# Two bursts of attention matmuls for each unit, and TensorE in the order in which the program is written

## The chip, the cores and the metric

The kernel runs on one core of a Trainium2 chip. The metric is device time in microseconds (us) of one execution: 988.76 us, the median of three runs (986.52 to 989.58). Five engines work side by side, each through its own queue in order: TensorE (PE in the profile, its weight loads PEld), VectorE (DVE), ScalarE (ACT), GpSimd (POOL) and SyncE (SP), which here issues the DMAs.

## The reference

Three stages follow each other on 3072 tokens (4 sequences of 768). Weights come as float64, everything else is float32.

```python
# attention: B, H, S, D = 4, 8, 768, 48; a state of 48x48 for each head, decayed channel by channel
for t in range(S):
    cur = einsum('bhd,bhe->bhde', u * k[t], v[t])
    y[t] = einsum('bhd,bhde->bhe', r[t], state + cur)
    state = w[t][..., None] * state + einsum('bhd,bhe->bhde', k[t], v[t])
x = y as [3072, 384]
x = ((x @ w1) * (x @ w2)) @ w3 @ w_out          # layer one: 384 -> 1024 -> 384
h = x @ w_in                                     # layer two: 384 -> 2048 -> 384
out = (h * clip(h + 3, 0, 6) / 6) @ w_out2
```

## The kernel before, in words

**Products.** A product of full precision is split into three matmuls of fp32r: high by high, high by low, low by high (`mm3`, L118 to L121). So almost every matmul of the trace has one of the lines L119, L120 and L121; its moving side has 384 columns in layer one and 512 in layer two. "A product" below is nine such matmuls, three for each 128 rows of the contraction.

**Start (0 to 116.6 us).** w3 and w_out are multiplied into one matrix (w34, L375) while the float64 words of the weights are turned into float32 by integer arithmetic on DVE, ACT and POOL (`conv`, `split`). The first units of attention run beside that.

**Attention** is cut into 32 units: a pair of heads, half a sequence, three chunks of 128 tokens. Head 0 of a pair lies on partitions 0 to 47, head 1 on 64 to 111. For unit m:

- `load(m)`: two DMAs, `wkr` (decays, k, r by channel) and `rkv` (r, k, v by token), into three buffers each; the load of unit m+2 waits until unit m-1, which had the buffer, is done.
- `prep(m)`: DVE scans the products of decays forwards (`e`, L154) and backwards (`f`, L158) and multiplies r and k by them (L168, L165); POOL and DVE make the diagonal of the scores (`A`).
- `do_kn`: PE transposes k (L186, "T" below). `do_sc(m, j)`: the scores of head j, three matmuls of 48 rows (L195, "SC"), which DVE then copies under a mask into `A` (copy_predicated, L196).
- `do_kv`: the update of the state (L206, "KV"), 128 rows and 48 columns for each head and chunk; then a scan over the chunks on DVE (`s`, L213).
- `do_y(m-1)`, one unit late: for each chunk, the masked products v by A (L228, "YA", 128 rows, 48 columns) and then r by the state (L231, "YS", 48 rows, 48 columns) on top of them, in one bank. A unit of a sequence's first half has no state in its first chunk, so it has two chunks of YS; one of the second half has three. y goes to `xt` in two or three DMAs.

The PSUM banks `abank` (three) go round: T, SC of head 0, SC of head 1, YA and YS, KV. So KV takes the bank that head 0's scores leave when copy_predicated has read them.

**Layer one (116.6 to about 583 us)** goes through eight blocks of 384 tokens. For each of eight feature tiles f there are two products into banks 0 and 1 (`ab`, weights w12), an elementwise product (`a`, L474), its split into `gh` and `gl`, and then `out1` for the tile before: nine matmuls into banks 2 to 4. Between these products, steps of attention for the next block are pulled: after each product the quota grows by 0.3 (0.5 in block 6), and each full one emits a whole unit's step, until the next block's four units are done. After feature tile 3 of block 6 attention is over; its memory goes to the weights of layer two (`win_start`), which are converted until layer two begins.

**Layer two** goes through six blocks of 512 tokens and 16 feature tiles: one product into bank 0 or 1, Relu on ACT, a multiplication on DVE, the split, and `out2` for the tile before (L506).

**What sets the order.** The kernel is built with a scheduler that simulates the engines and puts each engine's instructions into the order in which they come free there. It moves matmuls past each other: attention's matmuls stand in pieces between the products.

The DMA queue has one order too: SP issues loads, writes of y to `xt` and the rest, and waits at its head.

Of the kernel before, what the change touches and what calls it, by code (L numbers as in the profile page):

```python
# [16 lines left out]
NP = H // 2            # head pairs  # L17
T1 = S // 2            # tokens of a block of the first layer: half a sequence
NM = B * 2 * NP        # units of attention: a head pair, half a sequence
C = 128                # chunk of the recurrence  # L20
NC = T1 // C           # chunks in a unit
ZC = C + 1
WZ = NC * ZC + 1       # decay columns, with a zero column around each chunk
PR = 112               # head 0 of a pair on partitions 0..47, head 1 on 64..111
NS = NC + 2            # columns of the state scan: reset, carried state, chunks
# [3 lines left out]
T2 = 512               # tokens of a block of the second layer  # L29
NB2 = B * S // T2  # L30
NT = B * S
# limits of float64's upper word read as float32, for the two ways of conversion
# [4 lines left out]
TINY = 1e-25           # least product of decays within a chunk; less is held there and told by its reciprocal  # L37
FAR = 1e13             # largest reciprocal of a chunk's product of decays
PACE, PACE6 = 0.3, 0.5  # steps of attention for each product of the first layer; in its block 6
FW = 3                 # feature tile of block 6 after which attention's memory goes to the second layer  # L40


def pool_split(bi, f):
    """Where Pool takes a product's low part from the vector engine, which converts weights then."""
    return bi in (0, 1, 7) and f % 2 and f < 7


def build(nc, tc, a):
# [23 lines left out]
    count = cst.tile([1, 1], I32, name="count")  # L72
    half = cst.tile([128, 1], F32, name="half")
# [16 lines left out]
    # ------------------------------------------------------------ weights  # L90
    def conv(f, raw, late, mixed):
        """float64 words to float32, cut to 24 bits, in two stages; exponents beyond float32's are limited."""
# [30 lines left out]
    # ------------------------------------------------------------ attention  # L123
# [66 lines left out]
    def do_sc(m, j):  # L190
        d = un[m]
        ps = psum_a()[:, :T1].rearrange("p (c t) -> p c t", t=C)
        for c in range(NC):
            t = slice(C * c, C * c + C)
            mm(ps[:, c], d["k"][rows[j], t], d["r"][rows[j], t], start=True, stop=True)  # L195
        V.copy_predicated(d["A"][:, j], mask.unsqueeze(1).to_broadcast([128, NC, C]), ps)  # L196
# [23 lines left out]
    def do_y(m):  # L220
# [3 lines left out]
        pc = c3(ps)  # L224
        for c in range(NC):
            st = h > 0 or c > 0
            for j in range(2):
                mm(pc[rows[j], c], d["v"][:, c, j], d["A"][:, j, c], start=True, stop=not st)  # L228
            if st:
                for j in range(2):  # L230
                    mm(pc[rows[j], c], d["s"][rows[j], :, c + 1], d["r"][rows[j], C * c:C * c + C], start=False,  # L231
                       stop=True)
# [11 lines left out]
    def attention():  # L244
        for m in range(NM + 1):
            nxt = prep(m + 1) if m + 1 < NM else iter(())
            if m < NM:
                do_kn(m)
                next(nxt, None)
                do_sc(m, 0)  # L250
                do_sc(m, 1)
                next(nxt, None)
            if m + 2 < NM:
                load(m + 2)
            next(nxt, None)
            if m > 0:
                do_y(m - 1)
            if m < NM:
                do_kv(m)
            next(nxt, None)  # L260
            yield 4 * m + 4
# [4 lines left out]
    def pull(limit, k=1):  # L266
        """Emits up to k steps of attention; all of block `limit` ends with its step 4 * NP * (limit + 1) + 3."""
# [12 lines left out]
    # ------------------------------------------------------------ start  # L280
    raws, fs = {}, {}

    def w_load(key, src, n):
        """float64 words of a slice; src is [128, n] or [k, 128, n / k]."""
# [17 lines left out]
    class Stream:  # L302
        """Weight slices, each loaded, converted and split in turn."""
# [67 lines left out]
    # third and fourth weight as one  # L371
# [30 lines left out]
    # ------------------------------------------------------------ first layer  # L402
# [17 lines left out]
    def verdict():  # L420
        """Counts the channels whose decays the chunks can divide by."""
        ok = att.tile([PR, 2], F32, name="ok", bufs=1)
# [3 lines left out]
        V.memset(ok[:, 1:2], 1.0)  # L426
        ps = psum_a()[:1, :1]
# [3 lines left out]
    def win_start():  # L431
        verdict()
        close("att")
        p2["hp"] = pool("hp", bufs=2, side="left")
# [22 lines left out]

    prev = None
    quota = 0.0
    for bi in range(2 * B):  # L460
        x = xt[divmod(bi, 2)]
        for f in range(NF1):
# [27 lines left out]
            if bi == 7:  # L490
                p2["wi"].upto(2 * (7 - FW) + 2 * (f + 1))
# [7 lines left out]
    # ------------------------------------------------------------ second layer  # L499
    p2["wi"].upto(2)  # L500
    out1(*prev)

# [10 lines left out]
    prev = None  # L513
    for m in range(NB2):
        x = x1s.pop(m)
        for j in range(NF2):
# [7 lines left out]
            gh = p2["hp"].tile([128, T2], F32R, name=f"gh2_{m}_{j}", tag="gh2")  # L524
            gl = p2["hp"].tile([128, T2], F32R, name=f"gl2_{m}_{j}", tag="gl2")
# [3 lines left out]
            if prev is not None:  # L529
                out2(*prev)  # L530
# [182 lines left out]
```

## Time and profile before

| what | us |
|---|---|
| median of three runs | 988.76 |
| span of the profiled execution | 989.0 |
| PE busy in the span | 921.9 (93%) |
| DVE busy | 553.1 (56%) |
| ACT, POOL busy | 377.7, 248.7 |
| first product of layer one starts | 116.67 |
| last y of attention (DVE) | 503.07 |
| layer two without a stop from | 585.01 |
| last matmul starts | 981.22 |

The profile is one execution; its span is within the runs' range. PE is busy nearly all the time, but not with the same thing: until 116.6 us and again from 504 to 583 us DVE is the engine that is almost always busy, and between 187 and 504 us and after 583 us it is PE. A busy PE counts a matmul from its start to its modelled end, and matmuls overlap, so what one costs is read from start to start of neighbours. A float32 matmul of attention leaves two records in the trace, one of fp32r leaves one.

### The profile page before, as it was taken

What the parts mean: (1) busy time and instruction counts of PE and PEld (TensorE: products, weight loads), DVE (VectorE), ACT (ScalarE), POOL (GpSimd) and SP (SyncE); (2) the same over time, 40 slices, a digit from 0 to 9 for tenths busy, and PEclk for the clock granted to TensorE, in tenths of its full rate; (3) what the DMA queues carried; (4) which work ended last, traced back from release to release, by engine and by line L of the source; (5) the groups of instructions that cost most, each with busy time, mean ns of one, the idle gap of its engine ahead of it and who ended that gap; (6) DMA issues with size and microseconds to landing.
All of it is one profiled execution on the core that took longest, in us unless ns stands there. A gap on an engine that the chain in (4) does not pass through costs nothing.

```text
span 989.0 us, 13413 instructions
## 1 busy us (share of the span) xinstructions
PE 921.9 (93%) x5074; PEld 752.1 (76%) x5074; DVE 553.1 (56%) x938; ACT 377.7 (38%) x876; POOL 248.7 (25%) x297
## 2 busy tenths in 40 slices
PE   5888598999999999999998889999999999999997
PEld 3455377878788888879787878888888888888885
DVE  8999999664654745464469973333333423333332
ACT  5444454323233323232356552333333423432422
POOL 4888578241322313031125440000000000000000
PEclk9779699999999999999999999999999999999999
DMA  9675565450524325151225540010100000000001
GB/s 285 211 226 172 157 186 169 130 138 18 164 63 127 102 76 153 38 141 52 88 56 166 163 136 1 0 65 1 32 32 1 32 1 1 33 1 1 32 1 36
DMA packets 40761, 86.18 MB, mean 87 GB/s; under 512 B 4352, under 2 KB 20208, under 8 KB 40688
## 3 DMA queue, kind: packets, MB, share of 16 engines
q1 hardware_dynamic: 40688, 85.23, 28.7%
q8 instruction: 42, 0.69, 0.3%
q14 instruction: 31, 0.25, 0.1%
HBM read 66.34 MB, written 9.44 MB: 77 GB/s over the span
## 4 chain that ended last, share of the span: by engine, by line
PE 73%; DVE 15%; DMA 6%; issue 2%; ACT 2%; POOL 2%; SPq 0%; POOLq 0%; DVEq 0%; ACTq 0%
PE bank L119 22%; PE bank L120 21%; PE bank L121 21%; DMA wkr<-in_wkr 5%; PE abank L195 3%; PE abank L228 3%; PE abank L231 3%; DVE f L158 1%; PE abank L206 1%; DVE wkr L165 1%; DVE w3f L99 1%; DVE w3f L101 1%; PE abank L186 1%; DVE e L154 1%; DVE A L196 1%
## 5 line engine op out<-in xcount | busy, mean ns | idle before, releaser
L527 DVE SCALAR_TENSOR_TENSOR q<-q,bank 128x512 f32<-128x512 f32 x96 | 66.0, 688 | 163.6 <-ACT q L526 162.6
L119 PE MATMUL bank<-xt,w12h 128*128 128x384 f32 x384 | 138.4, 361 | 19.1 <-ACT kvs L211 11.7
L121 PE MATMUL bank<-xt,w12l 128*128 128x384 f32 x384 | 131.8, 343 | 0.0
L120 PE MATMUL bank<-xt,w12h 128*128 128x384 f32 x384 | 131.6, 343 | 0.0
L526 ACT ACTIVATE q<-bank,half 128x512 f32<-128x512 f32 x96 | 66.1, 689 | 154.6 <-PE bank L121 153.6
L116 DVE TENSOR_TENSOR gl<-q,gh 128x512 fp32r<-128x512 f32 x96 | 66.5, 693 | 91.7 <-ACT gh L115 78.5
L119 PE MATMUL bank<-x,wih 128*128 128x512 f32 x288 | 113.8, 395 | 1.5 <-DVE q L527 1.5
L121 PE MATMUL bank<-x,wil 128*128 128x512 f32 x288 | 114.1, 396 | 0.0
L120 PE MATMUL bank<-x,wih 128*128 128x512 f32 x288 | 113.9, 395 | 0.0
L121 PE MATMUL bank<-gh,w12l 128*128 128x512 f32 x288 | 113.0, 392 | 0.0
L120 PE MATMUL bank<-gl,w12h 128*128 128x512 f32 x288 | 113.0, 392 | 0.0
L115 ACT CAST gh<-q 128x512 fp32r<-128x512 f32 x96 | 59.6, 621 | 97.1 <-PE bank L121 62.8
L119 PEld LDWEIGHTS bank<-xt,w12h 128*128 128x128 f32 x384 | 73.8, 192 | 28.6 <-ACT kvs L211 11.9
L119 PE MATMUL bank<-gh,w12h 128*128 128x512 f32 x288 | 83.9, 392 | 0.0
L120 PEld LDWEIGHTS bank<-xt,w12h 128*128 128x128 f32 x384 | 73.9, 192 | 0.6
L121 PEld LDWEIGHTS bank<-xt,w12l 128*128 128x128 f32 x384 | 73.6, 192 | 0.9 <-issue 0.2
L175 POOL TENSOR_SCALAR_AFFINE_SELECT A<-sd 128x384 f32<-128x384 f32 x64 | 42.0, 678 | 117.4 <-PE abank L228 113.2
L120 PE MATMUL bank<-gl,w34h 128*128 128x384 f32 x192 | 66.8, 348 | 4.7 <-DVE gl L116 4.7
L121 PE MATMUL bank<-gh,w34l 128*128 128x384 f32 x192 | 66.0, 344 | 0.0
L119 PEld LDWEIGHTS bank<-x,wih 128*128 128x128 f32 x288 | 54.2, 188 | 14.7 <-DVE q L527 1.9
L154 DVE TENSOR_TENSOR_SCAN e<-wkr,d1c 112x388 f32<-112x388 f32 x32 | 36.6, 1144 | 50.8 <-DMA wkr<-in_wkr 50.8
L121 PEld LDWEIGHTS bank<-x,wil 128*128 128x128 f32 x288 | 54.1, 188 | 12.8
(128 smaller groups left out, 1653.9 us busy)
## 6 DMA issues: line engine op xcount, KB each, us to landing
wkr<-in_wkr SPq DMA_DIRECT2D x32, 505.8 KB, 5.7
rkv<-in_rkv SPq DMA_DIRECT2D x32, 432.0 KB, 4.0
raw_wo<-in_w_out SPq DMA_DIRECT2D x24, 384.0 KB, 3.5
raw_w<-in_w3T SPq DMA_DIRECT2D x15, 512.0 KB, 5.2
xt<-y SPq DMA_DIRECT2D x48, 144.0 KB, 4.7
raw_w<-in_w SPq DMA_DIRECT2D x16, 384.0 KB, 4.2
raw_wi<-in_w_in SPq DMA_DIRECT2D x16, 384.0 KB, 3.8
x1d<-x SPq DMA_DIRECT2D x8, 576.0 KB, 4.4
```

The source lines that it names most:

```text
L115: ACT.copy(hi, src)
L116: (eng or V).tensor_tensor(out=lo, in0=src, in1=hi.bitcast(F32), op=ALU.subtract)
L119: mm(ps, wh, xh, start=first, stop=False)
L120: mm(ps, wh, xl, start=False, stop=False)
L121: mm(ps, wl, xh, start=False, stop=last)
L154: V.tensor_tensor_scan(out=e, data0=d["w"], data1=d1c, initial=0.0, op0=ALU.mult, op1=ALU.max)
L175: P_.affine_select(out=A[:, j], in_=sd[:, :, j].unsqueeze(2).to_broadcast([128, NC, C]), pattern=[[0, NC], [-1, C]], compare_op=ALU.is_equ ...
L195: mm(ps[:, c], d["k"][rows[j], t], d["r"][rows[j], t], start=True, stop=True)
L228: mm(pc[rows[j], c], d["v"][:, c, j], d["A"][:, j, c], start=True, stop=not st)
L231: mm(pc[rows[j], c], d["s"][rows[j], :, c + 1], d["r"][rows[j], C * c:C * c + C], start=False, stop=True)
L526: ACT.activation(q, ps, AF.Relu, bias=half, scale=1.0 / 6.0)
L527: V.scalar_tensor_tensor(out=q, in0=q, scalar=1.0, in1=ps, op0=ALU.min, op1=ALU.mult)
```

## The change

- The scores of both heads are emitted together, heads in turn chunk by chunk, into two banks; T and SC form a first burst.
- In `do_y` the products with the state come first, for all chunks, then all masked products; then KV follows. That is the second burst. The order of accumulation in the bank is set by hand (`start` for the first matmul of each head).
- Attention yields after each burst, so a pulled step is half a unit. The quota is 0.45 half steps for each product (0.8 in block 6) in place of 0.3 (0.5) whole ones.
- From the first product of layer one to the last of layer two, PE keeps the order in which the program emits; the other engines and the start are scheduled as before.
- In layer two `out2` stands two tiles behind in place of one, with three buffers of `gh2` and `gl2`; their pool is opened after layer one's `gp` is closed.
- The one matmul that counts channels with extreme decays goes to block 7.

```diff
-PACE, PACE6 = 0.3, 0.5
+PACE, PACE6 = 0.45, 0.8
-    def do_sc(m, j):
+    def do_sc(m):
         d = un[m]
-        ps = psum_a()[:, :T1].rearrange("p (c t) -> p c t", t=C)
+        ps = [psum_a()[:, :T1].rearrange("p (c t) -> p c t", t=C) for _ in range(2)]
         for c in range(NC):
             t = slice(C * c, C * c + C)
-            mm(ps[:, c], d["k"][rows[j], t], d["r"][rows[j], t], start=True, stop=True)
-        V.copy_predicated(d["A"][:, j], mask.unsqueeze(1).to_broadcast([128, NC, C]), ps)
+            for j in range(2):
+                mm(ps[j][:, c], d["k"][rows[j], t], d["r"][rows[j], t], start=True, stop=True)
+        for j in range(2):
+            V.copy_predicated(d["A"][:, j], mask.unsqueeze(1).to_broadcast([128, NC, C]), ps[j])
...
+        started = [False, False]
+        def part(j, c, left, right):
+            mm(pc[rows[j], c], left, right, start=not started[j], stop=True, skip_group_check=True)
+            started[j] = True
+        for c in range(0 if h else 1, NC):
+            for j in range(2):
+                part(j, c, d["s"][rows[j], :, c + 1], d["r"][rows[j], C * c:C * c + C])
         for c in range(NC):
-            st = h > 0 or c > 0
             for j in range(2):
-                mm(pc[rows[j], c], d["v"][:, c, j], d["A"][:, j, c], start=True, stop=not st)
-            if st:
-                for j in range(2):
-                    mm(pc[rows[j], c], d["s"][rows[j], :, c + 1], d["r"][rows[j], C * c:C * c + C], start=False,
-                       stop=True)
+                part(j, c, d["v"][:, c, j], d["A"][:, j, c])
...
             if m < NM:
                 do_kn(m)
+                do_sc(m)
                 next(nxt, None)
-                do_sc(m, 0)
-                do_sc(m, 1)
                 next(nxt, None)
+            yield 4 * m + 2
             if m + 2 < NM:
                 load(m + 2)
-            next(nxt, None)
             if m > 0:
                 do_y(m - 1)
             if m < NM:
                 do_kv(m)
             next(nxt, None)
+            next(nxt, None)
             yield 4 * m + 4
...
+    order = tc.manual_schedule(engines={mybir.EngineType.PE})
+    order.__enter__()
     prev = None
     quota = 0.0
     for bi in range(2 * B):
...
     p2["wi"].upto(2)
     out1(*prev)
+    close("gp")
+    p2["hp"] = pool("hp", bufs=2, side="left")
...
-            if prev is not None:
-                out2(*prev)
-            prev = (m, j, gh, gl)
+            if len(late) == 2:
+                out2(*late.pop(0))
+            late.append((m, j, gh, gl))
```

PE, before: the matmuls of attention at the start of block 4 of layer one, two pieces (L186 is T, L195 SC, L228 YA, L231 YS, L206 KV; the matmuls of layer one between the pieces are left out).

```order
L186 MATMUL abank_67<-ident,wkr_3104 128x112 x2
L195 MATMUL abank_66<-wkr_3104 128x128
L195 MATMUL abank_68<-wkr_3104 128x128 x3
L195 MATMUL abank_66<-wkr_3104 128x128 x2
...
L228 MATMUL abank_67<-A_3137,rkv_2898 48x128 x2
L231 MATMUL abank_67<-wkr_2896,s_3245 48x128 x2
L228 MATMUL abank_67<-A_3137,rkv_2898 48x128 x2
L231 MATMUL abank_67<-wkr_2896,s_3245 48x128 x2
L228 MATMUL abank_67<-A_3137,rkv_2898 48x128 x2
L231 MATMUL abank_67<-wkr_2896,s_3245 48x128 x2
L206 MATMUL abank_68<-rkv_3106,kt_3288 48x48 x4
```

PE, after: the two bursts at about the same place (L187 is T, L198 SC, L234 YS with `wkr,s` and YA with `A,rkv`, L210 KV).

```order
L187 MATMUL abank_68<-ident,wkr_2953 128x112 x2
L198 MATMUL abank_66<-wkr_2953 128x128
L198 MATMUL abank_67<-wkr_2953 128x128
L198 MATMUL abank_66<-wkr_2953 128x128
L198 MATMUL abank_67<-wkr_2953 128x128
L198 MATMUL abank_66<-wkr_2953 128x128
L198 MATMUL abank_67<-wkr_2953 128x128
...
L234 MATMUL abank_68<-wkr_2845,s_3183 48x128 x6
L234 MATMUL abank_68<-A_2983,rkv_2847 48x128 x6
L210 MATMUL abank_66<-rkv_2955,kt_3218 48x48 x4
```

The scores' banks change with each matmul, YS and YA stand apart as six and six, and KV follows YA.

SP, before: the loads of unit m+2 and the writes of y after them, in layer one's block 5.

```order
L137 DMA rkv_3643<-in_rkv 128x864
L135 DMA wkr_3641<-in_wkr 112x1156
L241 DMA xt_0_3659<-y_3656 48x768 x2
L414 DMA x1d<-x_4_3701 384x1x384
L137 DMA rkv_3748<-in_rkv 128x864
L135 DMA wkr_3746<-in_wkr 112x1156
```

SP, after, at the same place.

```order
L136 DMA wkr_3672<-in_wkr 112x1156
L425 DMA x1d<-x_4_3667 384x1x384
L138 DMA rkv_3674<-in_rkv 128x864
L251 DMA xt_0_3689<-y_3686 48x768 x2
L136 DMA wkr_3783<-in_wkr 112x1156
L138 DMA rkv_3785<-in_rkv 128x864
```

`wkr` stood behind `rkv` and stands ahead of it now: its buffer is free after YS, that of `rkv` after YA.

PE, before: the end of layer one (`w34`) and the first matmuls of layer two (`wih`, `wil`).

```order
L121 MATMUL bank_65<-gh_6_5064,w34l 128x384
L119 MATMUL bank_61<-x_0_4941,wih 128x512
L120 MATMUL bank_61<-x_0_4941,wih 128x512
L121 MATMUL bank_61<-x_0_4941,wil 128x512
...
L120 MATMUL bank_62<-x_0_4941,wih 128x512
L121 MATMUL bank_62<-x_0_4941,wil 128x512
L119 MATMUL bank_63<-gh_7_5108,w34h 128x384
L119 MATMUL bank_64<-gh_7_5108,w34h 128x384
```

PE, after, at the same place.

```order
L122 MATMUL bank_65<-gh_6_5063,w34l 128x384
L120 MATMUL bank_63<-gh_7_5107,w34h 128x384
L121 MATMUL bank_63<-gl_7_5108,w34h 128x384
...
L121 MATMUL bank_65<-gl_7_5108,w34h 128x384
L122 MATMUL bank_65<-gh_7_5107,w34l 128x384
L120 MATMUL bank_61<-x_0_4940,wih 128x512
```

Before, the first two products of layer two (18 matmuls) stand ahead of the last nine of layer one; now they stand behind them.

## Rows read from the trace of the kernel before

**Rows 1.** Busy time of each engine by stage; columns stand in the second line.

```profile
core 0: us, PE busy (x) PEld busy (x) DVE busy (x) ACT busy (x) POOL busy (x), PEclk, DMA share, GB/s
0.00:116.60 116.60, 81.31 (x392) 47.71 (x392) 109.47 (x184) 55.54 (x144) 86.08 (x87) 0.86 0.72 220
116.60:187.00 70.40, 65.74 (x408) 55.57 (x409) 65.89 (x121) 33.43 (x92) 44.85 (x42) 0.91 0.56 167
187.00:504.00 317.00, 310.15 (x2211) 265.15 (x2210) 164.20 (x299) 98.52 (x313) 77.23 (x137) 0.99 0.33 93
504.00:583.00 79.00, 67.62 (x356) 62.31 (x355) 73.44 (x132) 48.39 (x104) 39.60 (x32) 0.98 0.46 141
583.00:981.00 398.00, 396.48 (x1712) 321.16 (x1711) 140.11 (x205) 140.55 (x224) 0.94 (x1) 1.00 0.05 18
```

**Rows 2.** Timeline of PE: start us, us, instruction, records, idle before.

```profile
300.48 0.33 PE L120 MATMUL bank<-xt,w12h 128*128 128x384 f32 x1
300.65 0.34 PE L121 MATMUL bank<-xt,w12l 128*128 128x384 f32 x1
300.92 0.42 PE L228 MATMUL abank<-A,rkv 128*48 128x128 f32 x2
301.27 0.45 PE L119 MATMUL bank<-xt,w12h 128*128 128x384 f32 x1
301.56 0.34 PE L120 MATMUL bank<-xt,w12h 128*128 128x384 f32 x1
...
303.06 0.43 PE L228 MATMUL abank<-A,rkv 128*48 128x128 f32 x4
303.42 0.46 PE L231 MATMUL abank<-wkr,s 48*48 48x128 f32 x4
303.81 0.42 PE L228 MATMUL abank<-A,rkv 128*48 128x128 f32 x4
304.17 0.46 PE L231 MATMUL abank<-wkr,s 48*48 48x128 f32 x4
304.56 0.47 PE L206 MATMUL abank<-rkv,kt 128*48 128x48 f32 x12
304.96 0.44 PE L119 MATMUL bank<-gh,w34h 128*128 128x384 f32 x1
```

**Rows 3.** Timeline of PE, transposes and scores, one head after the other.

```profile
309.79 0.45 PE L186 MATMUL abank<-ident,wkr 112*128 112x112 f32 x3
310.17 1.26 PE L195 MATMUL abank<-wkr 48*128 48x128 f32 x12
311.36 0.44 PE L119 MATMUL bank<-gh,w34h 128*128 128x384 f32 x1
```

**Rows 4.** Timeline of PE, scores that the scheduler put with heads in turn.

```profile
330.48 0.94 PE L195 MATMUL abank<-wkr 48*128 48x128 f32 x12
331.35 0.44 PE L121 MATMUL bank<-xt,w12l 128*128 128x384 f32 x1
```

**Rows 5.** Timeline of PE, a y with two chunks of YA together, and KV.

```profile
313.72 0.64 PE L228 MATMUL abank<-A,rkv 128*48 128x128 f32 x8
314.29 0.46 PE L231 MATMUL abank<-wkr,s 48*48 48x128 f32 x4
...
315.90 0.47 PE L206 MATMUL abank<-rkv,kt 128*48 128x48 f32 x12 [0.40 <-DVE A L196]
```

**Rows 6.** Busy time by stage of the instructions on layer one's banks alone.

```profile
187.00:504.00 317.00, 226.68 (x1169) 200.42 (x1168) 24.00 (x44) 28.76 (x61) 0.99 0.33 93
```

**Rows 7.** PE's waits, 187 to 504 us: waited for, us, times, longest.

```profile
PE abank L206 <- DVE A L196: 6.8, 5, 2.2
```

**Rows 8.** Timeline of DVE around the same unit.

```profile
311.72 0.97 DVE L154 TENSOR_TENSOR_SCAN e<-wkr,d1c 112x388 f32<-112x388 f32 x1 [5.41 <-DMA wkr<-in_wkr]
...
315.27 1.05 DVE L196 COPY_PREDICATED A<-mask,abank 128x384 f32<-128x384 int32 x2
```

**Rows 9.** Timeline of SP's DMA queue, the loads that this scan waits for.

```profile
304.31 0.33 SPq L137 DMA_DIRECT2D rkv<-in_rkv  x1
304.74 0.38 SPq L135 DMA_DIRECT2D wkr<-in_wkr  x1
```

More of the change, by code (lines that the diff above doesn't have):

```diff
@@ L72, in build @@
     count = cst.tile([1, 1], I32, name="count")
+    ok = cst.tile([PR, 2], F32, name="ok")
     half = cst.tile([128, 1], F32, name="half")
@@ L420, in verdict @@
     def verdict():
-        ok = att.tile([PR, 2], F32, name="ok", bufs=1)
         for i, most in enumerate((C + 1.0, FAR)):
@@ L426, in verdict, with verdict_count @@
         V.memset(ok[:, 1:2], 1.0)
+    def verdict_count():
         ps = psum_a()[:1, :1]
@@ L433, in win_start @@
         close("att")
-        p2["hp"] = pool("hp", bufs=2, side="left")
         wp = pool("wp", bufs=1, side="right")
@@ L490, in build @@
             if bi == 7:
+                if f == 2:
+                    verdict_count()
                 p2["wi"].upto(2 * (7 - FW) + 2 * (f + 1))
@@ L511, in out2 @@
                 nc.sync.dma_start(a["out"][ct, :, T2 * m:T2 * m + T2], t)
-    prev = None
+    late = []
     for m in range(NB2):
@@ L523, in build @@
             q = p2["hp"].tile([128, T2], F32, name=f"q_{m}_{j}", tag="q", bufs=4)
-            gh = p2["hp"].tile([128, T2], F32R, name=f"gh2_{m}_{j}", tag="gh2")
-            gl = p2["hp"].tile([128, T2], F32R, name=f"gl2_{m}_{j}", tag="gl2")
+            gh = p2["hp"].tile([128, T2], F32R, name=f"gh2_{m}_{j}", tag="gh2", bufs=3)
+            gl = p2["hp"].tile([128, T2], F32R, name=f"gl2_{m}_{j}", tag="gl2", bufs=3)
             ACT.activation(q, ps, AF.Relu, bias=half, scale=1.0 / 6.0)
@@ L534, in build @@
                     x1_load(m + 1)
-    out2(*prev)
-    for nm in ("hp", "gp", "x1p", "w12p", "wp", "xp", "stg"):
+    for held in late:
+        out2(*held)
+    order.__exit__(None, None, None)
+    for nm in ("hp", "x1p", "w12p", "wp", "xp", "stg"):
         close(nm)
```

## The prediction

> **What bounds the kernel now.** I read the busy time by stage first [rows 1]. Four stages have two different limits. Until 116.6 us DVE is busy 109.5 us, and from 116.6 to 187 us (layer one's first block, while w1 and w2 are still being converted) 65.9 of 70.4 us; from 504 to 583 us (attention is over, layer two's weights are converted) 73.4 of 79.0 us. There DVE sets the pace. From 187 to 504 us DVE is busy only 164 of 317 us and PE 310; after 583 us PE is busy 396.5 of 398 us. There PE sets the pace. The change moves PE's work, so it can pay in full only between 187 and 504 us.
>
> Next I read PE's timeline from start to start. A layer-one matmul takes 0.175 us (300.48 to 300.65) [rows 2]. Then 1169 of them [rows 6] are 204 us, and the other 106 us of PE's 310 in that stage are attention: about 22.5 units, so 4.7 us a unit. That is the price to bring down. How it comes about is in the same rows: two records of YA between products take 0.27 us to get going (300.65 to 300.92, 0.09 more than a product's cadence), 0.35 us until the next product, and the first product after them 0.29 us (301.27 to 301.56, 0.11 too much). So each piece of attention costs about 0.2 us beyond its own work, and the scheduler cuts a unit into several pieces. Inside a piece, changing between YA and YS costs too: four records of YA take 0.36 us with a change behind them, but eight take 0.57 [rows 5], so a chunk in the middle of a run costs 0.21 us, and the changes 0.15 to 0.18 each.
>
> **The change part by part.**
>
> *Scores with heads in turn.* One head after the other, twelve records take 1.19 us (310.17 to 311.36) [rows 3]. Once the scheduler happened to put the heads in turn into two banks, as the change always does, and the same twelve took 0.87 us [rows 4]. Gain 0.32 us a unit.
>
> *First burst now:* transposes 0.38 (309.79 to 310.17; entered without the extra 0.09, as they use nearly the full array) [rows 3], scores 0.87, first product afterwards 0.11: 1.36 us.
>
> *Second burst now:* entry 0.09; YS 0.39 for the first chunk, with its change [rows 2], and 0.21 for each further one. No row shows YS chunks in a row; the bounds are 0.21 (as YA, two heads side by side) and 0.39 (no gain from standing together), and I take 0.21, since with changes on both sides YS (0.39) and YA (0.36) cost almost the same. So 0.60 for two chunks, 0.81 for three. YA 0.57 + 0.21 = 0.78 for three chunks; KV 0.40 (304.56 to 304.96) [rows 2]; the product afterwards 0.11. Sum 1.98 or 2.19 us. With the first burst 3.34 and 3.55, less some 0.17 in units of a second half, which transpose and update one chunk less: about 3.36 us. How YA goes over to KV no row shows: between nothing gained and 0.15, the price of the cheaper change above, since both use 128 rows and 48 columns. I take 3.3 us a unit. The Trainium skill (TensorEngine Tiling (Array Packing), Key Properties) says that changing the tiling mode drains TensorE, changing the tile within a mode does not; by that YA to KV is free, and the sum would be 3.2. The steps between YA and YS agree with its first half; for the second, no row here shows a change of tile alone.
>
> *Fewer pieces* is contained in this: 3.3 is for exactly two bursts, 4.7 for what the scheduler made.
>
> *PE between 187 and 504 us.* The stretch from block 1 to the last y holds five blocks of 216 matmuls and 90 of block 6: 1170 times 0.1745 = 204 us. Attention there: units 9 to 31, and one y more, since before PE did unit 9's scores and the y of unit 8 ahead of 187 us and in program order it cannot: 23.5 units at 3.3 = 78 us. Waits: PE waited 6.8 us, for KV's bank alone [rows 7]; I keep 7. Sum 289 in place of 317: 28 us gained.
>
> *What those waits will be.* They come round a loop: y(m-1) frees `wkr`, SP loads it (304.74 to 311.72, 7.0 us), DVE stands with `e` at the head of its queue (idle 5.41 us), then `f`, `a`, k and copy_predicated (315.27), then KV has its bank (315.90, PE idle 0.40) [rows 5, 8, 9]. From y to KV that is 11 us. A unit now takes 1/(3 x 0.225) = 1.48 feature tiles of 27 matmuls, 7.0 us, and 3.3 of attention: 10.3 us; and KV stands behind y's 1.4 us. So 11.7 against 11 us: it just fits. One thing helps: `wkr` is now free after YS and is issued ahead of `rkv`, so its load starts by YA's 0.78 us and one issue, 0.43 us [rows 9], sooner against the end of y. Queued on DVE behind the waiting `e` are `a` and `gl`, for which PE waits two products later; two products and a burst are 4.4 us, about as long as `e` waits. POOL's `rn` products start up to 1 us later, with a unit's time to spare.
>
> *The start and block 0.* In program order PE cannot take units 5 and 6 ahead of the first product, so DVE has eight instructions fewer ahead of the first `a` in its order: 8 x 0.60 (109.47 / 184) [rows 1] = 5 us gained, if DVE is the limit. PE's need in block 0 falls to 216 x 0.175 + 4 x 3.3 = 51 us, but DVE's 65.9 us [rows 1] has as many instructions as before, so nothing more comes there. Bounds: 0 and the 14 us between 66 and 51 on top of the 5.
>
> *504 to 583 us.* DVE has the same work, and the last y stands at the same feature tile (3 of block 6). 79 us stay. PE no longer takes matmuls ahead while it waits for `gl`. PE is idle 11.4 us there [rows 1]; I take no more, and 11 more as the upper bound. But 18 matmuls of layer two stood ahead of layer one's last nine and filled idle time; some 16 of layer two's 1728 were over by 583 us, since 1712 are left [rows 1]. They now come afterwards: 16 x 0.232 (398 / 1712) = 3.7 us lost.
>
> *Layer two.* No gap to close: PE is busy 396.5 of 398 us [rows 1]. The lag of two tiles gains nothing over the order that the scheduler found of before. What it covers is the chain of ReLU, product and split behind each tile: in program order a lag of one leaves two products for it (18 x 0.232 = 4.2 us), a lag of two four (8.4 us). I count it at nothing; without any cover PE would stand for the whole chain at each of the 96 tiles.
>
> **Sum.** The span is 989.0 us, as good as the runs' median of 988.76. 989.0 - 28 - 5 + 3.7 = 959.7: 960 us.
>
> **The rivals.**
>
> *Waits in program order (slower).* The loop above does not close in time, and PE, which can no longer take a product ahead, stands at KV and at `ab` in each unit. For it: DVE idle 5.41 us at `e` [rows 8], and waits up to 2.2 us already [rows 7]. Against: five waits in over 20 units, and the earlier load. At 2.2 us for each of 27 units, 59 less the 7 counted: 960 + 52 = 1012 us. It decides from 1.3 us a unit on (36 / 27).
>
> *YS gains nothing from standing together*, as one bank takes both heads' partial sums: 0.18 us for each of 1.5 further chunks a unit, 27 units: 7 us; with the heads one after the other as well, 0.21 for 2.5 chunks, 14 more. 967 to 981, say 973 us. Against: YS with two changes costs as YA does. Beside it stands the Trainium skill (TensorEngine Tiling (Array Packing), Gotcha 1: PSUM Pressure): different row tiles cannot use the same PSUM bank at once. Four records of YS, two heads in one bank, in 0.39 us [rows 2] speak against a full price; the scores use two banks.
>
> *PE waits more while layer two's weights are converted*, since `out1` waits for `gl` with nothing behind it allowed past: up to the 11 us above: 971 us. For it: DVE is the limit there, so `gl` is late often. Against: then the scheduler's freedom did not help either.
>
> *Block 0 follows PE and not DVE:* up to 14 us less, 946 us. DVE's order there holds conversions of w_in that nobody waits for yet, so its 66 us are not all needed.
>
> **How the numbers follow.** Forecast 960: 0.52 (its own range 953 to 967). PE waits in 504 to 583: 0.14. YS: 0.12. Block 0: 0.13. Waits in program order: 0.09. A measurement of this kernel can tell 0.3%, 3 us, from no change. The first four hold 0.91 and stay under 986. Half of the waits' price would end at 986, and so might two of the bad cases together: 0.04 for within 0.3%, of which 0.03 come from those four and 0.01 from the waits; 0.08 for slower, 0.88 for faster. The range 943 to 980 leaves out the waits and the far ends.
>
> **What would show it.** Right: a unit's scores in 0.87 us, YA to KV without a step, about 3.3 us of PE a unit, first product near 112 us, last y near 470, last matmul near 952, layer two's cadence unchanged at 0.23 us. Wrong: PE waits for KV or `a` of over 1 us in most units; a first block that ends much before or after 181 us; more than 83 us from the last y to layer two's steady run.

## The result and the profile after

| | before | after |
|---|---|---|
| median of the runs, us | 988.6 (986.52 to 989.58, four runs) | 962.05 (960.99 to 963.34, four runs) |
| ratio, 95% interval | | 0.973 (0.9714 to 0.9746) |
| span of the profiled execution, us | 989.0 | 959.8 |
| first product of layer one | 116.7 | 110.7 |
| block 1's first `a` | 189.9 | 186.1 |
| block 6's first `a` | 475.6 | 444.0 |
| last y | 503.1 | 468.4 |
| layer two's 19th matmul | 585.0 | 558.0 |
| last matmul | 981.2 | 952.3 |

The marks are start times (us) in the two traces. The change made the kernel 2.7% faster; 960 us was forecast. Read from mark to mark, the five blocks from block 1 to block 6 give 27.7 us (285.7 to 257.9), the stretch until block 1 gives 3.8, the stretch from the last y to layer two's steady run takes 7.6 us back (81.9 to 89.6), and layer two itself gives 1.9 (396.2 to 394.3). The rest, 3.1 us, lies in block 6's share of attention (27.5 to 24.4).

Busy time by stage of the kernel after from its first product on, cut at nearly the same events as before (columns as in [rows 1]: length, then PE, its weight loads, DVE, ACT and POOL with their instructions, granted clock, DMA share, GB/s):

```profile
110.60:182.40 71.80, 57.81 (x403) 52.02 (x404) 67.02 (x121) 32.39 (x90) 40.97 (x43) 0.92 0.60 170
182.40:468.50 286.10, 281.17 (x2258) 261.26 (x2258) 175.35 (x305) 97.27 (x322) 90.24 (x142) 1.00 0.38 108
...
552.40:952.00 399.60, 399.60 (x1727) 325.73 (x1726) 139.41 (x204) 140.41 (x221) 0.00 (x0) 1.00 0.05 16
```

The second line carries the gain. Of it, the same view of layer one's banks alone:

```profile
182.40:468.50 286.10, 216.99 (x1169) 200.62 (x1169) 23.29 (x43) 29.09 (x62) 1.00 0.38 108
```

There are 1169 matmuls, exactly as many as in [rows 6]; at 0.1745 us from start to start they are 204 us. PE's waits in this stage (what waits for what: us, times, longest):

```profile
PE bank L120 <- DVE a L487: 1.5, 2, 1.3
...
PE abank L210 <- DVE A L200: 0.5, 1, 0.5
```

With the four lines left out they sum to 4.9 us. So attention has 286.1 - 204 - 4.9 = 77.2 us; by 23.5 units that is 3.28 us a unit, where 3.3 was forecast and 4.7 was the price before. The unit itself is in PE's timeline (start, us to the modelled end, instruction, records):

```profile
304.86 0.34 PE L122 MATMUL bank<-gh,w34l 128*128 128x384 f32 x1
305.12 0.68 PE L234 MATMUL abank<-wkr,s 48*48 48x128 f32 x8
305.74 0.86 PE L234 MATMUL abank<-A,rkv 128*48 128x128 f32 x12
306.49 0.47 PE L210 MATMUL abank<-rkv,kt 128*48 128x48 f32 x12
306.90 0.45 PE L120 MATMUL bank<-xt,w12h 128*128 128x384 f32 x1
307.18 0.34 PE L121 MATMUL bank<-xt,w12h 128*128 128x384 f32 x1
...
310.13 0.45 PE L187 MATMUL abank<-ident,wkr 112*128 112x112 f32 x3
310.52 0.94 PE L198 MATMUL abank<-wkr 48*128 48x128 f32 x12
311.38 0.45 PE L120 MATMUL bank<-gh,w34h 128*128 128x384 f32 x1
```

From start to start: 0.26 to get into the burst (0.09 more than a product), YS 0.62, YA 0.75, KV 0.41, the matmul of layer one afterwards 0.28 (0.11 too much); later T 0.39 and SC 0.86. The forecast had YS 0.60 for two chunks, YA 0.78, KV 0.40, T 0.38 and SC 0.87. In this unit KV starts a little late. In 17 of the 20 units of the five blocks YA takes 0.69 us, and KV 0.37 with 12 records (0.28 with 8), as here:

```profile
394.48 0.86 PE L234 MATMUL abank<-A,rkv 128*48 128x128 f32 x12
395.17 0.44 PE L210 MATMUL abank<-rkv,kt 128*48 128x48 f32 x12
395.54 0.44 PE L120 MATMUL bank<-xt,w12h 128*128 128x384 f32 x1
```

In the trace's single records the matmuls of YA start 0.109 us apart (medians over the five blocks), the first of KV starts 0.109 after the last of YA, and the first of YA 0.205 after the last of YS. So the passage to KV has no step of its own. That is the case of which no row of before told. The Trainium skill (TensorEngine Tiling (Array Packing), Key Properties) lets only a change of the tiling mode drain TensorE. The trace agrees: where the rows used change, from YS to YA, there is a step of some 0.10 us, and between YA and KV, which share rows and columns, there is none.

The loop that might have taken a wait's place, in DVE's timeline (in brackets the idle time before and what ended it):

```profile
310.40 0.97 DVE L155 TENSOR_TENSOR_SCAN e<-wkr,d1c 112x388 f32<-112x388 f32 x1 [0.54 <-DMA wkr<-in_wkr]
```

and in SP's queue:

```profile
305.85 0.34 SPq L136 DMA_DIRECT2D wkr<-in_wkr  x1
```

`wkr` is issued 0.11 us after YS ended its starts (305.74), ahead of `rkv`. From that issue to `e` it is 4.6 us, against 7.0 in [rows 8, 9], and DVE stands idle before `e` for 0.54 us in place of 5.41. But this unit is an extreme one. Over the kernel the median of `wkr` from issue to landing went from 5.7 to 4.6 us, and over the five blocks DVE's waits for it, before and after, are these:

```profile
DVE e L154 <- DMA wkr<-in_wkr: 43.7, 16, 5.6
DVE e L155 <- DMA wkr<-in_wkr: 36.5, 19, 3.5
```

So DVE still waits there in most units. The forecast had counted on 0.43 us from the earlier issue; the median load came 1.1 us quicker on top.

Outside that stage PE still waits. Its waits in block 0, between 110.6 and 182 us:

```profile
PE bank L121 <- DVE gl L117: 5.8, 2, 4.2
PE bank L120 <- ACT w12h L116: 5.4, 1, 5.4
PE abank L210 <- DVE A L200: 3.8, 3, 2.5
...
```

and between 468.5 and 553 us:

```profile
PE bank L121 <- DVE gl L117: 9.9, 6, 2.8
...
PE bank L120 <- DVE a L487: 1.5, 2, 1.2
...
```

For these two the kernel before has 4.1 and 5.0 us in 504 to 583 us. The same stretch as a whole, from the last y to layer two's 19th matmul, before and after:

```profile
503.10:585.00 81.90, 69.01 (x362) 63.36 (x360) 75.79 (x136) 50.08 (x108) 40.55 (x32) 0.98 0.45 139
468.40:558.00 89.60, 74.99 (x370) 69.38 (x369) 74.68 (x136) 51.60 (x110) 42.03 (x32) 0.92 0.44 140
```

PE is idle 14.6 us in place of 12.9, and busy 75.0 in place of 69.0, at a granted clock of 0.92 in place of 0.98. With two levels of the clock, 0.92 of 89.6 us means some 14 us at 1.2 GHz, and 0.98 of 81.9 some 3. The 8 more recorded matmuls are at most 1.6 us of it. So most of the 7.6 us lies in PE's busy time and not in its waits. Layer two begins at the lower clock, too:

```profile
552.37 0.63 PE L120 MATMUL bank<-x,wih 128*128 128x512 f32 x1
552.80 0.63 PE L121 MATMUL bank<-x,wih 128*128 128x512 f32 x1
...
555.63 0.40 PE L122 MATMUL bank<-x,wil 128*128 128x512 f32 x1
```

Seven matmuls start 0.43 us apart before the cadence of 0.235 is reached. The granted clock between 552.37 and 555.36 us is 0.50, the level of 1.2 GHz; in the 7 us ahead of 552 it was 1.00 and PE was busy 4.5 of them. That is 7 x 0.2 = 1.4 us of the 7.6.

### The profile page after: what moved, and what is told of

It is laid out like the page before. It is cut to its first block, busy times and chain, and to the rows that moved or that the text cites. A ratio compares the mean times of both kernels' runs of the same rounds, so it can differ in the third digit from the quotient of the medians.

```text
span 959.8 us, 13483 instructions
## 1 busy us (share of the span) xinstructions
PE 880.5 (92%) x5074; PEld 744.9 (78%) x5074; DVE 556.1 (58%) x938; ACT 374.3 (39%) x876; POOL 257.9 (27%) x297
## 4 chain that ended last, share of the span: by engine, by line
PE 69%; DVE 17%; DMA 7%; issue 2%; POOL 2%; ACT 2%; SPq 0%; ACTq 0%; POOLq 0%; DVEq 0%
PE bank L120 21%; PE bank L121 21%; PE bank L122 21%; DMA wkr<-in_wkr 4%; PE abank L234 3%; PE abank L198 2%; DVE f L159 1%; DMA raw_w<-in_w 1%; DVE e L155 1%; POOL w3f L104 1%; DMA raw_wo<-in_w_out 1%; DVE w12l L117 1%; DVE raw_w L101 1%; DVE a L487 1%; DVE wil L117 1%
## 5 line engine op out<-in xcount | busy, mean ns | idle before, releaser
L544 DVE SCALAR_TENSOR_TENSOR q<-q,bank 128x512 f32<-128x512 f32 x96 | 66.1, 688 | 193.7 <-ACT q L543 193.6
L120 PE MATMUL bank<-gh,w12h 128*128 128x512 f32 x288 | 112.2, 390 | 0.0
L386 PE MATMUL bank<-wo,w3f 128*128 128x384 f32 x128 | 55.7, 592 | 24.6 <-POOL w3f L104 17.7
L176 POOL TENSOR_SCALAR_AFFINE_SELECT A<-sd 128x384 f32<-128x384 f32 x64 | 45.3, 731 | 99.7 <-PE abank L234 89.8
L116 ACT CAST gh<-a 128x384 fp32r<-128x384 f32 x64 | 32.7, 510 | 93.6 <-DVE a L487 93.4
L120 PE MATMUL bank<-gh,w34h 128*128 128x384 f32 x192 | 67.3, 351 | 2.0 <-ACT gh L116 2.0
```

The costliest lines, as they stand in the source:

```text
L116: ACT.copy(hi, src)
L120: mm(ps, wh, xh, start=first, stop=False)
L176: P_.affine_select(out=A[:, j], in_=sd[:, :, j].unsqueeze(2).to_broadcast([128, NC, C]), pattern=[[0, NC], [-1, C]], compare_op=ALU.is_equ ...
L386: mm(ps, w3[:, 128 * f4:128 * f4 + 128], wo[:, j].bitcast(F32), start=j == 0, stop=j == NF1 - 1)
L544: V.scalar_tensor_tensor(out=q, in0=q, scalar=1.0, in1=ps, op0=ALU.min, op1=ALU.mult)
```

## The experiments

Each ratio is to runs of the kernel before on the same chip (medians 987.98, 988.85 and 990.59 us in the three sets of runs). The kernel after was run again with the second set: 961.95 us, 0.9722 (0.9688 to 0.9756), with 257.0 us for the five blocks (186.8 to 443.8). "Five blocks" below is always from block 1's first `a` to block 6's, 257.9 us after and 285.7 before.

> The changed kernel once more, as the measure for the three others of this call: 960 to 966 us by every theory.

**Scores head by head.**

```diff
-        for c in range(NC):
-            t = slice(C * c, C * c + C)
-            for j in range(2):
+        for j in range(2):
+            for c in range(NC):
+                t = slice(C * c, C * c + C)
```

> The changed kernel with one part undone: the scores of a unit are again three matmuls of head 0, then three of head 1, inside the same first burst. If what the change saves is TensorE's own time between 187 and 504 us, the scores cost 1.19 us in place of 0.87 us for each of 27 units: 8.6 us back, some 971 us against 962. If the attention bursts hide behind something else (DVE or the loads), the time stays at 962. The rival in between: only the units in blocks 1 to 6 pay, 23 units, 7.4 us, 969.5 us.

974.07 us, 0.9828 (0.9769 to 0.9886). Five blocks 263.7 us, 5.8 more, or 0.29 for each of 20 units. In PE's timeline:

```profile
308.53 1.26 PE L198 MATMUL abank<-wkr 48*128 48x128 f32 x12
309.73 0.44 PE L120 MATMUL bank<-xt,w12h 128*128 128x384 f32 x1
```

1.20 us for what takes 0.86 in turn. Most of the rest of the 12 us lies ahead of block 1, which began 7.5 us later (193.6); the scores of block 0's own four units are some 1.2 of that (4 x 0.29). The granted clock was 0.81 between 114.1 and 189.5 us where the kernel after had 0.92. Why it was lower in this run's block 0 these runs don't settle; the kernel after itself, run again, had 0.87 from its first product to block 1's first `a`, against 0.93 in its first trace.

**y chunk by chunk, as before.**

```diff
-        for c in range(0 if h else 1, NC):
-            for j in range(2):
-                part(j, c, d["s"][rows[j], :, c + 1], d["r"][rows[j], C * c:C * c + C])
         for c in range(NC):
+            st = h > 0 or c > 0
             for j in range(2):
-                part(j, c, d["v"][:, c, j], d["A"][:, j, c])
+                mm(pc[rows[j], c], d["v"][:, c, j], d["A"][:, j, c], start=True, stop=not st)
+            if st:
+                for j in range(2):
+                    mm(pc[rows[j], c], d["s"][rows[j], :, c + 1], ..., start=False, stop=True)
```

> The changed kernel with one part undone: y goes chunk by chunk again, masked products and then the state's, in the same second burst. By the prices of the kernel before and after, a unit of a first half costs 0.33 us more and one of a second half 0.70 us: some 0.5 us for 27 units, 14 us back, 976 us. In this kernel the load of wkr also stands behind that of rkv again, and its buffer is free only at the end of y; if that loop (load, scan, copy_predicated, KV) is what TensorE would wait for, 0.5 to 1 us a unit come on top: up to 1000 us. If changes between the two kinds of products cost nothing in sum, 962 us.

976.73 us, 0.9891 (0.9829 to 0.9953); five blocks 266.4 us, 8.5 more. PE's timeline shows the changes back again:

```profile
309.05 0.64 PE L240 MATMUL abank<-A,rkv 128*48 128x128 f32 x8
309.63 0.46 PE L243 MATMUL abank<-wkr,s 48*48 48x128 f32 x4
310.02 0.42 PE L240 MATMUL abank<-A,rkv 128*48 128x128 f32 x4
310.37 0.46 PE L243 MATMUL abank<-wkr,s 48*48 48x128 f32 x4
310.77 0.47 PE L210 MATMUL abank<-rkv,kt 128*48 128x48 f32 x12
```

1.72 us until KV against 1.37 in the kernel after: 0.35 us for two more changes. Of the three parts that were undone one by one this is the largest.

**PE ordered by the scheduler again,** everything else as after.

```diff
-    order = tc.manual_schedule(engines={mybir.EngineType.PE})
-    order.__enter__()
...
-    order.__exit__(None, None, None)
```

> The changed kernel without the fixed order: the scheduler puts TensorE's instructions in order everywhere. It makes 36 pieces of attention more than the two bursts a unit. At 0.2 us for each piece that is 7 us in layer one, and the matmuls of layer two that fill the waits around 580 us (3.7 us) come back: 965 us. If pieces cost more, since scores split from their pair lose their overlap too, up to 972 us. The rival: program order costs more in waits (block 0, 504 to 583 us) than it saves: under 958 us.

974.69 us, 0.9849 (0.9796 to 0.9901), 10 more than expected. Five blocks 264.2 us, 6.3 more. I counted pieces (runs of matmuls into attention's banks between two matmuls of layer one) in PE's timeline of the five blocks: 74 before, 41 after, 66 here. With the 0.2 us that a piece costs, 25 pieces are 5.0 us; the pieces themselves last 63.5 us in all against 59.8, and 9 recorded matmuls of layer one fewer fall between the marks (1.6 us): 5.0 + 3.7 - 1.6 = 7.1, near what was measured. What nobody had expected is block 0, from the first product on:

```profile
112.60:197.00 84.40, 73.41 (x417) 61.76 (x417) 70.47 (x126) 34.53 (x96) 49.87 (x48) 0.81 0.51 146
```

Block 1 begins at 201.1 us, 15 later than after, at a granted clock of 0.81. But the execution in the trace took 982.5 us, 7.8 more than the median, at a granted clock of 0.953 over its span, where the other four had 0.966 to 0.970. So part of the 15 us belongs to that one execution. The median is 12.7 us above the kernel after, and the five blocks account for 6.3 of them; that leaves some 6 us for all the rest, block 0 among it. That the fixed order gains there, against this scheduler's choice with the new pieces, is likely and not shown; the kernel before was at 189.9 us with the old ones.

**Program order alone,** put around the loops of the kernel before, without the other parts.

```diff
+    order = tc.manual_schedule(engines={mybir.EngineType.PE})
+    order.__enter__()
     prev = None
...
     out2(*prev)
+    order.__exit__(None, None, None)
```

> The kernel before with one part of the change alone: TensorE in program order, while each unit's step stays whole (transposes, scores, y, KV in one burst), at the old pace, with the old order of scores and y. 70 pieces of attention fewer than before at 0.2 us are 14 us, less 3.7 us of filling: 978 us if nothing waits. By the theory that KV's bank comes free only some 10 us after the y that frees the load (load, scan, copy_predicated), the whole unit in one burst leaves about 2 us between the scores and KV and a period of 9 us: 1 to 2.5 us of waiting for 27 units, 1005 to 1045 us. So slower than before by that theory, faster by the theory that fewer pieces are all that counts.

1012.83 us, 1.0249 (1.0213 to 1.0286): slower, as expected, but by another wait than the one named. In 189 to 508 us PE waits for KV's bank 1.4 us in all, and for this:

```profile
PE abank L228 <- ACT kt L188: 11.4, 10, 2.2
...
```

y(m-1) stands at once behind unit m's scores here, and its bank is the one that T(m) left; ACT has to copy `kt` out of it. One such place in ACT's timeline:

```profile
211.90 0.31 ACT L164 ACTIVATE sq<-wkr 112x128 f32<-112x128 f32 x1 [2.44 <-DMA wkr<-in_wkr]
...
213.72 0.44 ACT L188 COPY kt<-abank 128x336 f32<-128x336 f32 x1
```

and the piece of PE that waits for it:

```profile
214.22 0.70 PE L228 MATMUL abank<-A,rkv 128*48 128x128 f32 x8 [1.29 <-ACT kt L188]
```

ACT stands 2.44 us at `sq`, which waits for the next unit's load, and the copy is behind it. With the two bursts, 18 matmuls of layer one lie between T and y, and this wait is 0.2 us in the whole stage. By the marks the five blocks lose 5.1 us, at a granted clock of 0.96 (before 0.99), so the wait and the clock are not told apart there; 11.0 go in the last stretch (93.0 us against 81.9), where `gl` is waited for 10.4 us.

**The pace faster.**

```diff
-PACE, PACE6 = 0.45, 0.8
+PACE, PACE6 = 0.6, 1.0
```

> The changed kernel at the old pace: 0.6 half steps for each product (1.0 in block 6) in place of 0.45 (0.8). A unit then has 5.2 us of products and 3.1 us of attention, 8.3 us, less than the 10.4 us that pass in the trace after from the end of YS to the end of copy_predicated. By the theory of that loop TensorE waits at KV, some 1 to 2 us for each of 23 units: 985 to 1005 us, with waits of abank on DVE A growing from 4 to over 25 us. If the slower pace does nothing, 962 us.

965.97 us, 0.9782 (0.9732 to 0.9833): a miss, it costs only 4 us. The loop does not bind as a steady period. YS of one block:

```profile
241.73 0.90 PE L234 MATMUL abank<-wkr,s 48*48 48x128 f32 x12
...
249.68 0.90 PE L234 MATMUL abank<-wkr,s 48*48 48x128 f32 x12
...
258.54 0.90 PE L234 MATMUL abank<-wkr,s 48*48 48x128 f32 x12
...
261.44 0.39 PE L210 MATMUL abank<-rkv,kt 128*48 128x48 f32 x8 [1.20 <-DVE A L200]
...
269.58 0.90 PE L234 MATMUL abank<-wkr,s 48*48 48x128 f32 x12
```

7.95, 8.86 and 11.0 us. At the faster pace a block's four units are through before the block ends: eight half steps at 0.6 a product are 13 of its 16 products. That the loads issued meanwhile give the next block's first units a lead fits DVE's wait at `e`, which falls to 26.6 us over the five blocks (36.5 in the kernel after). Four units wait at KV, 5.5 us over the stage, and the five blocks take 6.5 us more. So the loop is near its limit, as forecast, but it has slack to spend.

**Layer two's output one tile behind in place of two.**

```diff
-            if len(late) == 2:
+            if len(late) == 1:
```

> The changed kernel with the output of layer two one tile behind in place of two, in program order. The chain from a tile's product to its split is some 3 us (0.69 + 0.69 + 0.62 + 0.69 us of busy time and the steps between), and two products (4.2 us) stand in between: no wait, 962 us within 1 us. If the lag of two is needed, TensorE waits at each of 96 tiles: at 0.2 us a tile 981 us.

964.98 us, 0.9751 (0.9699 to 0.9803): 3 us above the kernel after, where 1 at most was expected without waits, and far from 981. From layer two's 19th matmul to the last 395.8 us against 394.3, and in all of layer two PE waits for `gl` alone, 0.5 us. The second tile of lag is worth at most 1.5 us there, in five spacings at layer two's first and last tiles; all other matmuls start 0.2307 us apart in both.

**Less work on DVE.** The conversion of the weights leaves out its last step, the lowest three bits.

```diff
-            V.scalar_tensor_tensor(out=fi, in0=lo, scalar=29, in1=fi, op0=ALU.logical_shift_right, op1=ALU.bitwise_or)
```

> The changed kernel with less work on VectorE: the conversion of weights that goes by VectorE alone leaves out its last step, which puts in the lowest three bits of the fraction. These steps take 0.4 to 0.74 us each in the trace after; 14 of them stand ahead of block 1 in VectorE's order (some 9 us) and 9 between attention's end and layer two (some 6 us). If VectorE is the limit of the start with block 0 and of the second stretch, they shrink by about as much: 947 us, 950 with some of it lost. If waits between engines set these stretches, and not VectorE's work, less than 4 us in all: over 958 us.

953.22 us, 0.9633 (0.9591 to 0.9675). Most of the gain lies in one place. Block 0 and the last stretch by stage:

```profile
112.90:182.20 69.30, 58.17 (x403) 53.33 (x404) 63.98 (x112) 31.68 (x90) 37.71 (x42) 0.90 0.58 165
466.90:548.80 81.90, 70.75 (x369) 66.54 (x368) 68.48 (x123) 51.12 (x110) 43.02 (x32) 0.96 0.49 153
```

From the last y to layer two's 19th matmul it takes 81.9 us in place of 89.6, with DVE busy 68.5 us in place of 74.7: there DVE's work counts in full. Block 1 stands at 185.8 (186.1), but the first product came at 112.9 (110.7 after; 109.7 to 114.1 in the other runs with this start). From there to block 1's first `a` it takes 73.0 us, where the kernel after takes 75.4 and the six traces with the same block 0 lie between 75.4 and 77.3. So nine instructions fewer on DVE were worth some 2.5 us in block 0: its work counts there too, in part. For the start this run can't tell.

**Program order only until attention is over.** The fixed order ends where layer two's weights begin; from there the scheduler sets PE's order.

```diff
                 pull_all(7)
+                order.__exit__(None, None, None)
                 win_start()
```

> The changed kernel with TensorE's fixed order ended when attention ends; the scheduler orders the rest of layer one and layer two. By the theory that the fixed order costs only what TensorE can no longer fill in there, the stretch from the last y to layer two's steady run falls by the matmuls of layer two that fill waits, 3.7 us: 958 us. If the fixed order itself makes TensorE wait for gl (9.9 us of it in the trace after, 4.1 before), up to 7 us less: 955 us. If the scheduler's order costs as much as it saves, 962 us.

959.18 us, 0.9705 (0.9667 to 0.9743). The last stretch takes 85.7 us in place of 89.6, a gain of the size of the forecast's fill:

```profile
465.30:551.00 85.70, 71.75 (x370) 66.20 (x368) 77.95 (x137) 51.85 (x111) 41.85 (x32) 0.96 0.45 140
```

Beside the same row of the kernel after, PE's idle time falls by 0.7 us only (14.6 to 13.9), and its busy time for the same 370 matmuls by 3.2, at a granted clock of 0.96 in place of 0.92. So the filling of waits is not shown to be what gave the 3.9 us. This run has the lowest median of a complete kernel here, but its interval overlaps that of the kernel after, so it can't be called faster than that.

**Sixteen subtractions of the low parts from DVE to POOL,** alone and with the edit before.

```diff
-                            None if j % 2 else P_) for j in range(NF2)])
-        p2["wo"] = Stream([(f"wo2_{j}", ..., None if j % 2 else P_)
+                            P_) for j in range(NF2)])
+        p2["wo"] = Stream([(f"wo2_{j}", ..., P_)
```

> The changed kernel with the low parts of layer two's weights all made on GpSimd: 16 subtractions of 0.86 to 1.07 us leave VectorE (15 us) and come to GpSimd at about 1.5 us each (24 us, beside 42 of 84 us in the stretch). By the theory that VectorE is the limit from attention's end to layer two, that stretch falls from 84 us towards TensorE's 69 us: by 8 to 13 us, 949 to 954 us. If GpSimd becomes the limit, or chains between engines set the stretch, less than 3 us, or slower.

> Both of the two other edits of this call together: if they act on different things, their gains add, 945 to 952 us; since both shorten the same stretch, and TensorE has 61 us of matmuls and 4 of layer two to put there, not under 943 us.

965.92 us, 0.9761 (0.9724 to 0.9798), and with both edits 967.47 us, 0.9781 (0.9735 to 0.9827): two misses in the same direction. The last stretch with POOL's larger share, from the last y to layer two's 19th matmul:

```profile
470.60:563.50 92.90, 75.42 (x369) 69.76 (x369) 77.67 (x120) 51.25 (x111) 54.08 (x48) 0.91 0.43 135
```

DVE does 16 instructions fewer than after (120 against 136) and is busy 3.0 us longer (77.7 against 74.7 us). The 16 had taken 15.3 us there (8.4 and 6.9 us), so its other instructions grew by some 18 us in all. Groups of DVE in this stretch (count, busy us, mean ns), with the sixteen moved:

```profile
L117 DVE TENSOR_TENSOR gl<-a,gh 128x384 fp32r<-128x384 f32 x10 | 9.2, 916 | 1.3 <-ACT gh L116 1.3
...
L113 DVE SCALAR_TENSOR_TENSOR f_wi<-raw_wi,f_wi 128x384 int32<-128x384 int32 x5 | 6.0, 1202 | 0.0
...
L108 DVE TENSOR_SCALAR f_wi<-f_wi 128x384 f32<-128x384 f32 x5 | 3.4, 676 | 0.0
```

The same groups of the kernel after:

```profile
L117 DVE TENSOR_TENSOR gl<-a,gh 128x384 fp32r<-128x384 f32 x10 | 6.3, 632 | 0.6 <-ACT gh L116 0.6
...
L113 DVE SCALAR_TENSOR_TENSOR f_wi<-raw_wi,f_wi 128x384 int32<-128x384 int32 x5 | 2.7, 547 | 0.0
...
L108 DVE TENSOR_SCALAR f_wi<-f_wi 128x384 f32<-128x384 f32 x5 | 1.7, 349 | 0.0
```

The same operation on the same shapes takes 632 ns beside a POOL that is busy 42.0 us of the stretch and 916 ns beside one that is busy 54.1; the second goes from 547 to 1202, the third from 349 to 676. Not every group grew: `f_wi` at L102 stays at 546 to 548 ns. In the trace each `gl` of over 1.1 us lies beside a POOL instruction for at least two thirds of its time, and those without one take 0.55 us. So what was taken off DVE came back as longer instructions. The Trainium skill (SBUF — State Buffer, Who interferes with whom) says that a DVE instruction with two inputs in SBUF contends with a GpSimd instruction that reads SBUF. The first two groups are of that kind and agree with it; the third has one input and grew as well.

## Why the prediction was right, step by step

- **The unit's price: right.** 3.28 us where 3.3 was taken. The three parts, each undone alone, cost 5.8 (scores), 8.5 (order in y) and 6.3 us (PE's order) over the five blocks, 20.6 of the 27.7 gained. The forecast had for the scores 0.32 x 20 = 6.4 us. The other 7.1 have no run of their own; some of it is pieces (74 before, 66 with the scheduler and the new code: 8 x 0.2 = 1.6). From another side: pieces last 79.6 us before and 59.8 after, 19.8 less, and 33 fewer of them at 0.2 are 6.6, so about 26.4 of 27.7 are attention's own. For YA and KV together the sum had 1.18 us, with up to 0.15 less if the passage gained; 1.06 came in most units. The prediction says that no row of before shows a change of tile alone; YA's own records in [rows 5] do, since the two heads take turns at different columns, at 0.21 us a chunk.
- **187 to 504 us: right.** From block 1's first `a` to the last y 30.9 us gained (313.2 to 282.3) for the 28 of the sum. Of the 2.9 between them 2.1 are waits, 4.9 us for the 7 taken.
- **The loop: right that it fits.** It was forecast to fit by 0.7 us. PE's waits at KV fell from 6.8 to 0.5 us; `wkr` landed 1.1 us sooner after its issue by the median, and DVE's waits at `e` only shrank (43.7 to 36.5 us over the five blocks), which costs PE nothing as long as KV is in time. The rival of waits in program order did not come about here. It did with program order alone, at another place: y's bank, through ACT. That a unit in two bursts gives ACT the time of 18 matmuls for `kt` was in no step of the forecast.
- **YS in one bank: the rival is out.** 8 records, two heads in one bank, in 0.62 us; less the 0.39 of a first chunk that is 0.23 for the second, close to the 0.21 taken. Further matmuls of YS start 0.109 us apart, as those of YA do.
- **Start and block 0: size nearly right, the reason for block 0 failed.** 5 us were forecast, 3.8 were left at block 1: 6.0 by the first product, then block 0 took 2.2 us more than before (75.4 in place of 73.2, to block 1's first `a`), where the step had it unchanged because DVE sets its pace. Nine DVE instructions fewer gave some 2.5 us there, so DVE's work counts, but it doesn't set the pace alone: it is busy 67.0 of 71.8 us, hardly more than before (65.9), and PE's idle time from the first product to block 1's first `a` grew from 4.6 to 13.9 us. What the trace shows are few, long waits for `gl`, `w12h` and A, and in a fixed order nothing behind them may go ahead. With the scheduler block 0 was longer still in the one execution traced. Which chain would have to be shortened stays open.
- **After the last y: direction right, the term too small.** 3.7 us of lost fill were forecast; by layer two's 19th matmul 7.6 were lost, 5.7 by the last matmul (478.1 to 483.8 from the last y). 89.6 us is more than the 83 that the prediction named as a sign of being wrong. Ending the fixed order at this point gave 3.9 back, the size of the fill, but most of it stands in PE's busy time. PE's idle time grew by 1.7 us over before: 9.9 us of waits for `gl` in place of 4.1, a part of the rival that had a chance of 0.14, less 3.5 of waits for `a`. The larger share is busy time and goes with the lower clock (granted 0.92, before 0.98), a term that the sum did not have. What brought the clock down, the waits or the order, no run here separates.
- **Layer two: right.** No gap to close. From its 19th matmul on it is 1.9 us shorter, and none of that is a wait: the 1.5 us that PE stood before lie ahead of that matmul, and within the stretch 1708 matmuls start 0.2318 us apart before and 0.2307 after. With a lag of one it is 0.2307 too, so the lag is not the reason; what is stays open.

By the marks the sum was -30.9 - 3.8 + 5.7 = -29.0 us where it had been set up as -28 - 5 + 3.7 = -29.3: errors of 2.9, 1.2 and 2.0 us that cancel to 0.3. The total is better than its terms, and that part of it is luck.

## What to carry to other kernels

Price attention-like small matmuls from start to start, and count the changes of shape: here each change between operand shapes cost 0.15 to 0.18 us and each piece between full products 0.2 (0.09 on the way in, 0.11 on the way out), and grouping, not doing less, made the 2.7%. Fix an engine's order only together with an order that leaves time behind each producer: the same fixed order cost 2.5% with the units whole and was worth 6.3 us over five blocks with the units in two bursts. Before work is moved to an idle engine, read how long the receiving and the giving engine's instructions are when both are busy.

## What the runs showed of the hardware that was not expected

- Several of DVE's instructions became 1.4 to 2.2 times as long (632 to 916 ns, 547 to 1202, 349 to 676) when POOL took more of the same work beside them, and DVE's busy time grew although 16 instructions had left it.
- Of the two loads of a unit, the one issued first lands sooner. `wkr` takes 4.6 us (median over the kernel) where it stands first and 5.7 where it stood second, while `rkv` went from 4.0 to 6.0; y chunk by chunk, which puts `rkv` first again, has 5.9 and 3.8. The order of two issues moved the landing by more than the issue's own 0.33 us.
- Layer two's first seven matmuls ran at half the clock though PE had been at the full clock, busy 4.5 of 7.0 us, just ahead of them.
- The granted clock of one stretch differs between executions of the same code: 0.93 and 0.87 in block 0 of the kernel after.
